# One kernel, three edits at once: LN1 reordered over eight PSUM banks, the spectral filter in three planes with its sums on VectorE, and the down weights issued after the LN2 norms

## Chip, cores, metric

One core of one Trainium2 chip. The metric is device microseconds of one execution; every time quoted is a median of runs that were all in the fast state. Profiles are single executions with the hardware profiler; their spans lie about 2 us under the timed runs. Engine names in the profile: PE is TensorE, PEld its weight loads, DVE VectorE, ACT ScalarE, POOL GpSimd, SP the engine that issues most DMAs. PS is PSUM, to whose banks the matmuls of these profiles write. "Lnnn" is a source line of the kernel that was profiled; the same statement has another number in another kernel.

## The reference

```python
h  = x + irfft2(rfft2(layernorm(x)) * (w_r + 1j*w_i))        # x: 2048 x 576, bf16
h2 = h + (gelu(n @ w_gate) * (n @ w_up)) @ w_down            # n = layernorm(h), hidden size 4608
```

## The kernel before

The kernel builds its own dependence graph: `P.op(engine, instruction, r=keys read, w=keys written)` appends an instruction to an engine's list in program order and makes it wait, by semaphores, for the last writers and readers of its keys. It runs in four stages: LN1 with the first half of the DFT along the sequence (`a_mm`, into `U`); a loop over 16 frequency groups, called D/B/V here; the inverse transform ("I") with LN2; and the gate/up and down matmuls.

The filter step of the loop, per group, complex product Y times W:

```python
# st_D(i): 6 matmuls; ACT copies the even half to ES; two DVE ops (line "CUS") make sums and differences
# st_B(i-2): 6 matmuls, ACT copies the result to YS [re, im], then:
ze = POOL if i < NG - 3 else DVE
for t_, T_, w_ in (("T1", T1, slice(0, 2)), ("T2", T2, slice(1, None, -1))):
    P.op(DVE, ... tensor_tensor(T_[:, sl], YS[:, sl], WS[:, g, w_], op=ALU.mult) ...)      # 580 elements each
for z, (t_, T_, op_) in enumerate((("T1", T1, ALU.subtract), ("T2", T2, ALU.add))):
    P.op(ze, ... tensor_tensor(ZS[:, z4, z], T_[:, sl, 0], T_[:, sl, 1], op=op_) ...)      # 290 elements each
# st_V(i-5): 6 matmuls on ZS, ACT copies the result to V
```

LN1's scale factor is multiplied into the DFT table (`ATS = ATB / std`). The 512 KB table comes in one DMA between the second and the third load of x. The weights are issued by two engines, and GpSimd's list runs in this order:

```python
... the ZS sums of the loop ...
for j in range(4):                        # gate: POOL queue, up: SP queue
    P.dma(POOL, WGU[... gate, chunk j ...]); P.dma(SP, WGU[... up, chunk j ...])
for j in range(9):
    P.dma(POOL, WD[:, 4*j:4*j+4, :], ...)                     # down weights
... in the I stage: norm(1, POOL), norm(3, POOL), then PE transposes (turn_pe) of the normed rows
```

## Time and profile before

| | before |
|---|---|
| timed median | 505.4 us (505.0 to 505.85) |
| profiled span | 503.9 us |
| first D matmul (end of LN1) | 22.49 us |
| first I matmul (end of the loop) | 56.01 us |
| loop, difference of the two | 33.52 us |
| from there to the end ("the rest") | 447.89 us |

The page of the kernel before, its chain of waits: the work that ended last, followed back, as shares of the span by engine and by line.

```profile
## 4 chain that ended last, share of the span: by engine, by line
PE 92%; DVE 4%; ACT 2%; DMA 1%; issue 1%; SPq 0%; DVEq 0%; ACTq 0%
```

TensorE holds almost all of it, and from the first I matmul on it is the limit nearly throughout. So the three times in this table decide everything here: first D, first I, and the rest. TensorE's timeline before gives them. Columns: start, duration of the merged entry, engine, line, operation, output and inputs, count, and in brackets the idle time before it and its releaser.

```profile
22.49 2.41 PE L548 MATMUL PS<-FT,U 128*128 128x290 bf16 x18 [0.35 <-DVE U L477]
...
47.12 0.91 PE L548 MATMUL PS<-FT,U 128*128 128x290 bf16 x6
...
56.01 0.41 PE L649 MATMUL PS<-DT,V 128*128 128x289 bf16 x2
```

The second line is the last D; in between, TensorE repeats every 1.91 us once all three steps run. VectorE's timeline of one group of the loop before:

```profile
28.93 0.45 DVE L554 TENSOR_TENSOR CUS<-ES,PS 128x290 bf16<-128x290 f32 x1
29.30 0.45 DVE L555 TENSOR_TENSOR CUS<-ES,PS 128x288 bf16<-128x288 f32 x1
29.66 0.45 DVE L578 TENSOR_TENSOR T_79<-YS,WS 128x580 bf16<-128x580 bf16 x1
30.03 0.92 DVE L578 TENSOR_TENSOR T_80<-YS,WS 128x580 bf16<-128x580 bf16 x1
30.88 0.45 DVE L554 TENSOR_TENSOR CUS<-ES,PS 128x290 bf16<-128x290 f32 x1
```

Read the starts, not the durations: an instruction of 0.45 us lets the next start after 0.37. The group takes 30.88 - 28.93 = 1.95 us. The second product is twice as long as the first, 0.92 us, for the same shape; GpSimd ran a sum beside it:

```profile
29.68 0.96 POOL L581 TENSOR_TENSOR ZS<-T_80 128x290 bf16<-128x290 bf16 x1
```

GpSimd's list later in the same run:

```profile
59.27 6.71 POOL L206 DMA_DIRECT2D WD<-in_B_w_down_dram  x9
66.01 6.17 POOL L715 TENSOR_SCALAR HN<-XO,TM,RS_59 128x576 bf16<-128x576 bf16 x4
```

The two norms start as soon as the nine DMAs have been issued.

### The profile page before, as it was taken

Reading aid. Unit: us, or ns where it says so; the run is one execution under the profiler, and the core shown is the slowest. Engines: PE = TensorE matmul, PEld = TensorE weight load, DVE = VectorE, ACT = ScalarE, POOL = GpSimd, SP = SyncE. Lnnn points to the kernel's source line nnn. Section 1 sums busy time; section 2 is a strip of 40 time slices with the busy share of each in tenths; the row PEclk is TensorE's granted clock in tenths of the full one; section 3 lists DMA queues with packets and bytes.
Section 4 is the critical chain, followed back from the end, with each engine's and each line's share of the span. In section 5 each row is a group of like instructions: output and inputs, shape, how many; then the busy total and the mean of one; then the engine's idle time right before and its main releaser. Section 6 shows DMA issues by size and latency. Waiting matters only on the chain.

```text
span 503.9 us, 10005 instructions
## 1 busy us (share of the span) xinstructions
PE 493.4 (98%) x4323; PEld 299.4 (59%) x4324; DVE 183.2 (36%) x382; ACT 157.1 (31%) x296; POOL 46.5 (9%) x61
## 2 busy tenths in 40 slices
PE   6899999999999999999999999999999999999998
PEld 2587675444457764444477754444577644444775
DVE  4899773344331014343310134333211233333111
ACT  5888776663220002323200022323100132323000
POOL 3278870000000000000000000000000000000000
PEclk9999999999999999999999999999999999999999
DMA  8679799001100000100000001100000000000000
GB/s 291 158 225 330 235 325 324 3 1 27 25 4 14 18 19 17 22 17 1 2 7 18 19 15 22 23 4 1 1 18 19 13 1 1 1 2 1 12 19 19
DMA packets 25661, 28.65 MB, mean 57 GB/s; under 512 B 11536, under 2 KB 19600, under 8 KB 25488
## 3 DMA queue, kind: packets, MB, share of 16 engines
q1 hardware_dynamic: 23040, 17.39, 11.9%
q0 software_dynamic: 2576, 10.62, 6.4%
q8 instruction: 34, 0.56, 0.5%
q14 instruction: 11, 0.09, 0.1%
HBM read 23.66 MB, written 2.36 MB: 52 GB/s over the span
## 4 chain that ended last, share of the span: by engine, by line
PE 92%; DVE 4%; ACT 2%; DMA 1%; issue 1%; SPq 0%; DVEq 0%; ACTq 0%
PE PS L783 56%; PE PS L806 28%; PE PS L649 2%; PE PS L548 2%; PE PS L688 2%; DMA XO<-in_A_x_dram 1%; DVE T_80 L578 1%; PE PS L568 1%; PE PS L595 1%; ACT U L479 1%; DVE T_79 L578 1%; DVE U L477 1%; DVE CUS L554 1%; ACT JNK L414 0%; DVE CUS L555 0%
## 5 line engine op out<-in xcount | busy, mean ns | idle before, releaser
L795 ACT ACTIVATE GL<-PS 128x512 bf16<-128x512 f32 x144 | 85.9, 597 | 289.3 <-PE PS L783 288.5
L796 DVE TENSOR_TENSOR AT<-GL,PS 128x512 bf16<-128x512 bf16 x144 | 98.9, 688 | 174.2 <-PE PS L783 172.5
L783 PE MATMUL PS<-HT_69,WGU 64*128 64x512 bf16 x1296 | 143.2, 376 | 0.0
L783 PE MATMUL PS<-HT_84,WGU 64*128 64x512 bf16 x1296 | 143.1, 376 | 0.0
L806 PE MATMUL PS<-WD,AT 128*128 128x288 bf16 (+2 forms) x1152 | 141.8, 286 | 0.0
L806 PEld LDWEIGHTS PS<-WD,AT 128*128 128x128 bf16 x1152 | 111.0, 98 | 31.5 <-issue 1.7
L783 PEld LDWEIGHTS PS<-HT_84,WGU 64*128 64x128 bf16 x1296 | 69.6, 94 | 71.6 <-issue 0.5
L783 PEld LDWEIGHTS PS<-HT_69,WGU 64*128 64x128 bf16 x1296 | 69.9, 94 | 70.8 <-issue 0.7
L809 DVE TENSOR_TENSOR OS<-PS,XO 128x288 bf16<-128x288 f32 (+2 forms) x32 | 14.6, 458 | 125.8 <-PE PS L806 125.8
L691 DVE SCALAR_TENSOR_TENSOR XO<-PS,XO 128x576 bf16<-128x576 f32 x16 | 12.1, 756 | 8.3 <-PE PS L688 8.3
L649 PE MATMUL PS<-DT,V 128*128 128x289 bf16 x96 | 14.6, 287 | 0.2 <-ACT V L603 0.2
L548 PE MATMUL PS<-FT,U 128*128 128x290 bf16 x96 | 14.3, 286 | 0.4 <-DVE U L477 0.4
L595 PE MATMUL PS<-VT,ZS 128*128 128x256 bf16 x96 | 13.4, 272 | 1.1 <-DVE CUS L555 0.4
L578 DVE TENSOR_TENSOR T_80<-YS,WS 128x580 bf16<-128x580 bf16 (+2 forms) x17 | 13.5, 794 | 0.0
L581 POOL TENSOR_TENSOR ZS<-T_80 128x290 bf16<-128x290 bf16 x13 | 12.2, 938 | 1.9
L606 ACT ACTIVATE V<-PS 128x768 bf16<-128x768 f32 x15 | 12.1, 810 | 0.8 <-PE PS L595 0.8
L571 ACT ACTIVATE YS<-PS 128x578 bf16<-128x578 f32 x16 | 10.5, 655 | 4.1 <-PE PS L568 3.7
L466 PE MATMUL PS<-ATS,XO 128*128 128x128 bf16 (+1 forms) x80 | 7.0, 233 | 4.6 <-POOL ATS L445 3.8
L421 DVE BATCH_NORM_STATS2 ST_53<-XO 128x6 f32<-128x288 bf16 x24 | 9.4, 442 | 4.9 <-DMA XO<-in_A_x_dram 4.9
L658 ACT ACTIVATE GS<-PS 128x578 bf16<-128x578 f32 x15 | 9.8, 654 | 4.2 <-PE PS L649 4.1
L568 PE MATMUL PS<-CUS,BT 128*128 128x289 bf16 (+2 forms) x96 | 10.8, 247 | 0.2 <-ACT YS L571 0.2
L649 PEld LDWEIGHTS PS<-DT,V 128*128 128x128 bf16 x96 | 8.9, 97 | 3.5 <-ACT V L603 0.5
(63 smaller groups left out, 190.8 us busy)
## 6 DMA issues: line engine op xcount, KB each, us to landing
WD<-in_B_w_down_dram POOLq DMA_DIRECT2D x9, 576.0 KB, 19.8
WGU<-in_B_w_up_dram SPq DMA_DIRECT2D x4, 1152.0 KB, 12.5
WGU<-in_B_w_gate_dram POOLq DMA_DIRECT2D x4, 1152.0 KB, 10.2
out_dram<-OS SPq DMA_DIRECT2D x30, 72.0 KB, 1.6
XO<-in_A_x_dram SPq DMA_DIRECT2D x3, 576.0 KB, 7.7
IT<-c_itab SPq DMA_DIRECT2D x1, 1024.0 KB, 5.5
HT_84<-HN SPq DMA_TRANSPOSE x40, 2.4
XO<-in_A_x_dram SPq DMA_DIRECT2D x2, 288.0 KB, 3.1
```

What stands on the lines that cost most here:

```text
L548: P.op(PE, lambda t, b=b, o=o, dt=dt, us=us, g=g: t.matmul(bank(b, 0, 128, 0, 2 * HK), U[:, us, g, :, :], FT[:, o, dt, :], start=(dt == 0) ...
L568: P.op(PE, lambda t, b=b, tb=tb, pl=pl, q0=q0, q1=q1, m=m, s3=s3, sp_=sp_: t.matmul(bank(b, 0, 128, q0, q1), BT[:, sp_, tb, :], CUS[:, s3, ...
L578: P.op(DVE, lambda v, g=g, sl=sl, q0=q0, q1=q1, T_=T_, w_=w_: v.tensor_tensor(T_[:, sl, :, q0:q1], YS[:, sl, :, q0:q1], WS[:, g, w_, q0:q1 ...
L581: P.op(ze, lambda v, sl=sl, z4=z4, z=z, T_=T_, op_=op_, q0=q0, q1=q1: v.tensor_tensor(ZS[:, z4, z, q0:q1], T_[:, sl, 0, q0:q1], T_[:, sl, ...
L595: P.op(PE, lambda t, b=b, o=o, c=c, zp=zp, sl=sl, sp_=sp_: t.matmul(bank(b, 0, 128, o, o + 256), ZS[:, sl, zp, 128 * c:128 * c + 128], VT[ ...
L606: P.op(ACT, lambda a, g=g, src=src: a.activation(V[:, :, :, g, :], src, ACTF.Copy), r=[("PS", bs[0]), ("PS", bs[2]), "Vfree"], w=[("V", g, ...
L649: P.op(PE, lambda t, b=b, h=h, i=i, kt=kt, c=c: t.matmul(bank(b, 0, 128, 0, K2), V[:, kt, c, :, :], DT[:, 3 * h + i, 0:K2], start=(i == 0) ...
L783: op = P.op(PE, lambda t, h0=h0, kt=kt, wt=wt, f=f, b=b, HT=HT, s=(half == 0 and j in (0, 5)), e=(half == 1 and j in (3, 8)): t.matmul(ban ...
L795: P.op(ACT, lambda a, s2=s2, b0=b0: a.activation(GL[:, s2, :], bank(b0), ACTF.Gelu_apprx_tanh), r=[("PS", b0)], w=[("GL", s2)])
L796: P.op(DVE, lambda v, s2=s2, b0=b0, f=f: v.tensor_tensor(AT[:, f, :], GL[:, s2, :], bank(b0 + 1), op=ALU.mult), r=[("GL", s2), ("PS", b0 + ...
L806: P.op(PE, lambda t, b=b, d0=d0, d1=d1, f=f, p=p: t.matmul(bank(b, 0, 128, 0, d1 - d0), AT[:, f, 128 * p:128 * p + 128], WD[:, f, d0:d1], ...
L809: P.op(DVE, lambda v, b=b, d0=d0, d1=d1, p=p, c=c: v.tensor_tensor(OS[:, p % 2, d0:d1], bank(b, 0, 128, 0, d1 - d0), XO[:, c, d0:d1], op=A ...
```

## The change

Intent: (1) start LN1 earlier and finish it sooner; (2) take GpSimd out of the filter loop, so that its sums no longer slow the products, and shorten the pipeline by one group; (3) free space and GpSimd time by loading weights in another order. With a stored plane -w_i the real part, `yr*wr - yi*wi`, becomes a sum like the imaginary part, so that one add does both. The core of the diff, with cuts (also changed, and not shown: the filter loads bring w_i before w_r, and the filler matmuls and PSUM banks of the last groups differ):

```diff
@@ x and table loads: the table in three pieces
-    for i, (c0, c1) in enumerate(((0, 2), (2, 4), (4, 8), (8, 12), (12, 16))):
-        P.dma(SP, XO[:, c0:c1, 0:D], ...)
-        if i == 1:
-            P.dma(SP, ATB[...], dram["ATAB"][:, :], "atb", w=["ATB"])
+    x_load(0, 0, 2)
+    x_load(1, 2, 4)
+    atb_load(0, 0, 4)
+    x_load(2, 4, 8)
+    atb_load(1, 4, 8)
+    x_load(3, 8, 12)
+    x_load(4, 12, 16)
+    atb_load(2, 8, 16)
@@ LN1 (cut: the whole order of its instructions is rewritten; five groups instead of six)
-        b = (5 * i + k) % 7
+        b = (5 * i + AORD.index(k) + 7) % 8
@@ st_D: wait only for the part of U that a matmul reads
-                     r=ukeys + ["FT"], w=[("PS", b)])
+                     r=uk[us] + ["FT"], w=[("PS", b)])
@@ filter: planes -w_i, w_r, w_i; one add of 580 elements on VectorE
+            for t_, w_ in enumerate((slice(1, None, -1), slice(2, 0, -1))):
+                P.op(DVE, ... tensor_tensor(TP[:, sl, t_], YS[:, sl], WS[:, g, w_], op=ALU.mult) ...)
+            P.op(DVE, ... tensor_tensor(ZS[:, z3], TP[:, sl, :, 0], TP[:, sl, :, 1], op=ALU.add) ...)
@@ before the loop: the plane -w_i
+    for i in range(NG):
+        P.op(POOL, lambda v, g=GORD[i]: v.tensor_scalar(WS[:, g, 0, :], WS[:, g, 2, :], -1.0, None, op0=ALU.mult), ...)
@@ loop: V one group sooner
-    for i in range(NG + 5):
+    for i in range(NG + 4):
...
-        if i >= 5:
-            st_V(i - 5)
+        if i >= 4:
+            st_V(i - 4)
@@ weights: the nine WD DMAs move from in front of the I stage to behind it; filter planes share
@@ memory with gate/up chunks 2 and 3, which therefore wait for the end of the filter
-    for j in range(9):
-        P.dma(POOL, WD[:, 4 * j:4 * j + 4, :], ...)
...
+    for j in range(9):
+        P.dma(POOL, WD[:, 4 * j:4 * j + 4, :], ...)
```

More of the change, by code (lines that the diff above doesn't have):

```diff
@@ L305, in _build @@
     XO = sb.alloc("XO", [128, NT, D], BF16)
-    WGU = sb.alloc("WGU", [128, 9, FF], BF16)
+    wgu_off = (sb.off + 63) // 64 * 64
+    WGU = sb.alloc("WGU", [128, 4, 9, FF // 4], BF16)
+    wgu_end = sb.off
+    sb.off = wgu_off + 2 * 9 * (FF // 4) * 2
+    WS = sb.alloc("WS", [128, NG, 3, KW], BF16)
+    sb.off = wgu_end
     HN = sb.alloc("HN", [128, 4, 640], BF16)
@@ L322, in _build @@
     U = sb.alloc("U", [128, 5, NG, NT, 8], BF16)
-    WS = sb.alloc("WS", [128, NG, 2, KW], BF16)
     CUS = sb.alloc("CUS", [128, 3, 2, KW], BF16)
@@ L350, in _build @@
     t1_off = sb.off
-    T1 = sb.alloc("T1", [128, 2, 2, KW], BF16)
-    T2 = sb.alloc("T2", [128, 2, 2, KW], BF16)
-    ZS = sb.alloc("ZS", [128, 4, 2, ZW], BF16)
+    TP = sb.alloc("TP", [128, 2, 2, 2, KW], BF16)
+    ZS = sb.alloc("ZS", [128, 3, 2, ZW], BF16)
     sb.off = t1_off
@@ L376, in _build, with x_load, atb_load @@
     ov = out[0].rearrange("(p c) d -> p c d", c=NT)
-    for i, (c0, c1) in enumerate(((0, 2), (2, 4), (4, 8), (8, 12), (12, 16))):
+    tabs = dram["ATAB"].rearrange("p (c k) -> p c k", c=NT)
+    def x_load(i, c0, c1):
         P.dma(SP, XO[:, c0:c1, 0:D], xv[:, c0:c1, :], f"x{i}", w=[("X", c) for c in range(c0, c1)])
-        if i == 1:
-            P.dma(SP, ATB[:, :, :].rearrange("p a b -> p (a b)"), dram["ATAB"][:, :], "atb", w=["ATB"])
+    def atb_load(i, c0, c1):
+        P.dma(SP, ATB[:, c0:c1, :], tabs[:, c0:c1, :], f"atb{i}", w=[("ATB", c) for c in range(c0, c1)])
+    x_load(0, 0, 2)
[6 more added lines that the diff above has]
+    atb_load(2, 8, 16)
     P.dma(SP, FT[:, :, :, :].rearrange("p a b c -> p (a b c)"), dram["FTAB"][:, :], "ft", w=["FT"])
@@ L389, in w_loads @@
         for jj in range(4):
-            o.append((WS[jj:64:4, g0:g1, pl, 1:K2], 1 + (16 * jj + g0) * K2, [[128 * K2, 16], [K2, g1 - g0], [1, K2 - 1]], jj))
-            o.append((WS[64 + jj:128:4, g0:g1, pl, 1:K2], 1 + (64 + 16 * jj + 16 - g0) * K2, [[128 * K2, 16], [-K2, g1 - g0], [1, K2 - 1]], 4 + jj))
+            o.append((WS[jj:64:4, g0:g1, 1 + pl, 1:K2], 1 + (16 * jj + g0) * K2, [[128 * K2, 16], [K2, g1 - g0], [1, K2 - 1]], jj))
+            o.append((WS[64 + jj:128:4, g0:g1, 1 + pl, 1:K2], 1 + (64 + 16 * jj + 16 - g0) * K2, [[128 * K2, 16], [-K2, g1 - g0], [1, K2 - 1]], 4 + jj))
         if hf:
             for p0 in range(2):
-                o.append((WS[64 * p0:64 * p0 + 64, 0, pl, 1:K2], 1 + 64 * p0 * K2, [[128 * K2, 16], [16 * K2, 4], [1, K2 - 1]], 8 + p0))
+                o.append((WS[64 * p0:64 * p0 + 64, 0, 1 + pl, 1:K2], 1 + 64 * p0 * K2, [[128 * K2, 16], [16 * K2, 4], [1, K2 - 1]], 8 + p0))
         return [lambda d=d, off=off, ap=ap, h=h: P.dma(eng, d, bass.AP(src.tensor, off, ap), f"w{pl}{hf}", r=["Wz"], w=[("W", hf, pl, h)]) for d, off, ap, h in o]
-    for f in w_loads(0, 0, SP) + w_loads(1, 0, SP) + w_loads(0, 1, SP) + w_loads(1, 1, SP):
+    for f in w_loads(1, 0, SP) + w_loads(0, 0, SP) + w_loads(0, 1, SP) + w_loads(1, 1, SP):
         f()
@@ L407, in _build, with act_sum, act_sq @@
     P.op(POOL, lambda g: g.memset(ZS[:, :, :, K2:ZW], 0.0), w=["Zz"])
-    GROUPS = ((0, 2), (2, 4), (4, 8), (8, 12), (12, 14), (14, 16))
-    ACT_TILES = (3, 7, 11, 13)
-    def ln1_act(c):
+    GROUPS = ((0, 2), (2, 4), (4, 8), (8, 12), (12, 16))
+    ACT_TILES = (1, 3, 7, 11, 13)
+    def act_sum(c):
         P.op(ACT, lambda a, c=c: a.activation(JNK[:, 0, :], XO[:, c, 0:D], ACTF.Identity, accum_out=SA[:, 0, c:c + 1]),
              r=[("X", c)], w=[("SA0", c), "J0"])
+    def act_sq(c):
         P.op(ACT, lambda a, c=c: a.activation(JNK[:, 1, :], XO[:, c, 0:D], ACTF.Square, accum_out=SA[:, 1, c:c + 1]),
@@ L439, in ln1_sqrt, with ln1_rs @@
              r=[("MV1", c) for c in range(c0, c1)] + ["EPT"], w=[("SD1", i)])
+    def ln1_rs(i):
+        c0, c1 = GROUPS[i]
+        P.op(DVE, lambda v, c0=c0, c1=c1: v.reciprocal(RS1[:, c0:c1], RS1[:, c0:c1]), r=[("SD1", i)], w=[("RS1", i)])
     def ln1_scale(i, eng):
         c0, c1 = GROUPS[i]
-        P.op(DVE, lambda v, c0=c0, c1=c1: v.reciprocal(RS1[:, c0:c1], RS1[:, c0:c1]), r=[("SD1", i)], w=[("RS1", i)])
         if eng == POOL:
@@ L446, in ln1_scale @@
                                                                RS1[:, c0:c1].unsqueeze(2).to_broadcast([128, c1 - c0, 128]), op=ALU.mult),
-                 r=[("RS1", i), "ATB"], w=[("ATS", c) for c in range(c0, c1)])
+                 r=[("RS1", i)] + [("ATB", c) for c in range(c0, c1)], w=[("ATS", c) for c in range(c0, c1)])
         else:
@@ L450, in ln1_scale, with a_bank, idle_mm @@
                 P.op(DVE, lambda v, c=c: v.tensor_scalar(ATS[:, c, :], ATB[:, c, :], RS1[:, c:c + 1], None, op0=ALU.mult),
-                     r=[("RS1", i), "ATB"], w=[("ATS", c)])
-    def idle_mm(n):
+                     r=[("RS1", i), ("ATB", c)], w=[("ATS", c)])
+    AORD = (0, 1, 4, 2, 3)
+    def a_bank(i, k):
+        return (5 * i + AORD.index(k) + 7) % 8
+    def idle_mm(n, i):
+        b = a_bank(i, AORD[0])
         for _ in range(n):
-            P.op(PE, lambda t: t.matmul(bank(7), ZD[:, 0:128], ZD[:, :], start=True, stop=True), r=["ZD"], w=[("PS", 7)])
+            P.op(PE, lambda t, b=b: t.matmul(bank(b), ZD[:, 0:128], ZD[:, :], start=True, stop=True), r=["ZD"], w=[("PS", b)])
     TILES = (slice(0, 256, 2), slice(256, 512, 2), slice(1, 256, 2), slice(257, 512, 2), slice(512, D))
@@ L461, in a_mm @@
         c0, c1 = GROUPS[i]
-        b = (5 * i + k) % 7
+        b = a_bank(i, k)
         w = 128 if k < 4 else 64
@@ L471, in a_ev @@
         n = c1 - c0
-        b = (5 * i + k) % 7
+        b = a_bank(i, k)
         w = 128 if k < 4 else 64
@@ L479, in a_ev, with a_mms, a_evs @@
             P.op(ACT, lambda a, s=src, d=dst: a.activation(d, s, ACTF.Copy), r=[("PS", b)], w=[("U", i, k)])
-    def a_group(i, engs, between=None, at=5):
-        for k in range(5):
+    def a_mms(i):
+        for k in AORD:
             a_mm(i, k)
-            a_ev(i, k, engs[k])
-            if k == at:
-                between()
+    def a_evs(i, eng, ks):
+        for k in ks:
+            a_ev(i, AORD[k], eng)
     P.op(ACT, lambda a: a.activation(SA[:, 0, 0:1], EPT[:, 0:1], ACTF.Sqrt), r=["EPT"], w=[("SA0", 0)])
-    A5 = (ACT,) * 5
@@ L490, in _build @@
-    ln1_act(3)
-    idle_mm(18)
+    idle_mm(11, 0)
+    act_sum(1)
+    act_sq(1)
     ln1_tile(0)
-    ln1_tile(1)
+    ln1_tile(2)
+    act_sum(3)
     ln1_var(0)
     ln1_sqrt(0)
-    ln1_act(7)
-    ln1_tile(2)
+    act_sq(3)
+    ln1_rs(0)
     ln1_scale(0, DVE)
+    a_mms(0)
     ln1_var(1)
     ln1_sqrt(1)
+    a_evs(0, ACT, (0, 1, 2, 3, 4))
+    ln1_rs(1)
+    ln1_scale(1, DVE)
+    idle_mm(2, 1)
+    a_mms(1)
     ln1_tile(4)
-    ln1_scale(1, POOL)
-    a_group(0, A5)
-    ln1_act(11)
@@ L505, in _build @@
     ln1_tile(5)
     ln1_tile(6)
+    act_sum(7)
+    act_sq(7)
+    a_evs(1, ACT, (0, 1))
     ln1_var(2)
     ln1_sqrt(2)
-    idle_mm(1)
-    a_group(1, A5)
-    ln1_act(13)
+    a_evs(1, ACT, (2, 3, 4))
     ln1_tile(8)
+    ln1_rs(2)
     ln1_scale(2, POOL)
+    idle_mm(7, 2)
+    a_mms(2)
+    act_sum(11)
+    act_sq(11)
     ln1_tile(9)
     ln1_tile(10)
+    act_sum(13)
     ln1_var(3)
     ln1_sqrt(3)
+    act_sq(13)
     ln1_tile(12)
-    ln1_var(4)
-    ln1_scale(3, POOL)
-    idle_mm(5)
@@ L522, in _build @@
-    a_group(2, A5, lambda: ln1_sqrt(4), 2)
-    ln1_tile(14)
-    ln1_scale(4, POOL)
-    ln1_tile(15)
-    ln1_var(5)
-    idle_mm(4)
-    a_group(3, (ACT, DVE, ACT, DVE, ACT), lambda: ln1_sqrt(5), 0)
-    ln1_scale(5, DVE)
-    a_group(4, (ACT, DVE, ACT, DVE, ACT))
-    a_group(5, (DVE, ACT, DVE, ACT, DVE))
-    idle_mm(2)
-    ukeys = [("U", i, k) for i in range(len(GROUPS)) for k in range(5)] + ["Uz"]
+    ln1_rs(3)
+    ln1_scale(3, POOL)
+    ln1_tile(14)
+    a_evs(2, ACT, (0, 1, 2))
+    ln1_tile(15)
@@ new lines, in _build @@
+    ln1_var(4)
+    a_evs(2, DVE, (4,))
+    ln1_sqrt(4)
+    ln1_rs(4)
+    ln1_scale(4, DVE)
+    a_evs(2, ACT, (3,))
+    idle_mm(4, 3)
+    a_mms(3)
+    a_evs(3, ACT, (0,))
+    a_evs(3, DVE, (1,))
+    a_evs(3, ACT, (2,))
+    a_evs(3, DVE, (3,))
+    a_evs(3, ACT, (4,))
+    a_mms(4)
+    a_evs(4, DVE, (0,))
+    a_evs(4, ACT, (1,))
+    a_evs(4, ACT, (2,))
+    a_evs(4, DVE, (3,))
+    a_evs(4, ACT, (4,))
+    uk = [[("U", i, k) for i in range(len(GROUPS))] + ["Uz"] for k in range(5)]
+    ukeys = [k for ks in uk for k in ks]
@@ L563, in st_B @@
         s3, sp_ = i % 3, 1 if g == 0 else 0
-        b0 = {1: 6, LAST: 2}.get(i, 4)
+        b0 = {1: 6, LAST - 1: 2}.get(i, 4)
         for b, tabs in ((b0, (0, 1, 3)), (b0 + 1, (1, 2, 0))):
@@ L571, in st_B @@
         P.op(ACT, lambda a, sl=sl, b0=b0: a.activation(YS[:, sl, :, 0:K2], banks(b0, 2, K2), ACTF.Copy), r=[("PS", b0), ("PS", b0 + 1)], w=[("Y", sl)])
-        wk = wkeys[0 if 1 <= g < 9 else 1] + ["Wz", "Yz", "Zz"]
-        z4 = i % 4
-        ze = POOL if i < NG - 3 else DVE
+        wk = wkeys[0 if 1 <= g < 9 else 1] + [("Wn", i), "Yz", "Zz"]
+        z3 = i % 3
         for q0, q1, hs in ((0, 128, (0,)), (128, KW, (1,))) if i == LAST else ((0, KW, (0, 1)),):
-            for t_, T_, w_ in (("T1", T1, slice(0, 2)), ("T2", T2, slice(1, None, -1))):
-                P.op(DVE, lambda v, g=g, sl=sl, q0=q0, q1=q1, T_=T_, w_=w_: v.tensor_tensor(T_[:, sl, :, q0:q1], YS[:, sl, :, q0:q1], WS[:, g, w_, q0:q1], op=ALU.mult),
-                     r=[("Y", sl)] + wk, w=[(t_, sl, h) for h in hs])
-            for z, (t_, T_, op_) in enumerate((("T1", T1, ALU.subtract), ("T2", T2, ALU.add))):
-                P.op(ze, lambda v, sl=sl, z4=z4, z=z, T_=T_, op_=op_, q0=q0, q1=q1: v.tensor_tensor(ZS[:, z4, z, q0:q1], T_[:, sl, 0, q0:q1], T_[:, sl, 1, q0:q1], op=op_),
-                     r=[(t_, sl, h) for h in hs], w=[("Z", z4, z, h) for h in hs])
-    VBANKS = {NG - 5: (0, 0, 1), NG - 3: (0, 0, 1), NG - 2: (4, 4, 5), LAST: (6, 7, 2)}
+            for t_, w_ in enumerate((slice(1, None, -1), slice(2, 0, -1))):
+                P.op(DVE, lambda v, sl=sl, g=g, q0=q0, q1=q1, t_=t_, w_=w_: v.tensor_tensor(TP[:, sl, t_, :, q0:q1], YS[:, sl, :, q0:q1], WS[:, g, w_, q0:q1], op=ALU.mult),
+                     r=[("Y", sl)] + wk, w=[("T", sl, t_, h) for h in hs])
+            P.op(DVE, lambda v, sl=sl, z3=z3, q0=q0, q1=q1: v.tensor_tensor(ZS[:, z3, :, q0:q1], TP[:, sl, :, 0, q0:q1], TP[:, sl, :, 1, q0:q1], op=ALU.add),
+                 r=[("T", sl, t_, h) for t_ in range(2) for h in hs], w=[("Z", z3, h) for h in hs])
+    VBANKS = {NG - 4: (0, 0, 1), NG - 2: (2, 2, 3), LAST: (0, 1, 4)}
     def st_V(i):
         g = GORD[i]
-        sl = i % 4
+        sl = i % 3
         sp_ = 1 if g == 0 else 0
@@ L596, in st_V @@
                                                                                   VT[:, sp_, zp, :], start=(zp == 0), stop=(zp == 1)),
-                     r=[("Z", sl, z, int(c > 0)) for z in range(2)] + ["Zz", "VT"], w=[("PS", b)])
+                     r=[("Z", sl, int(c > 0)), "Zz", "VT"], w=[("PS", b)])
             if i == LAST:
@@ L610, in idle_ft @@
             P.op(PE, lambda t, b=b: t.matmul(bank(b, 0, 128, 0, 2 * HK), FT[:, 0, 0, 0:128], FT[:, 0, 0, :], start=True, stop=True), r=["FT"], w=[("PS", b)])
-    P.alias(["ATB", "J0", "J1", "ZD"] + [("ATS", c) for c in range(NT)], ["Vfree"])
-    for i in range(NG + 5):
+    P.alias(["J0", "J1", "ZD"] + [(n_, c) for n_ in ("ATB", "ATS") for c in range(NT)], ["Vfree"])
+    for i in range(NG):
+        P.op(POOL, lambda v, g=GORD[i]: v.tensor_scalar(WS[:, g, 0, :], WS[:, g, 2, :], -1.0, None, op0=ALU.mult),
+             r=[k for k in wkeys[0 if 1 <= GORD[i] < 9 else 1] if k[2] == 1] + ["Wz"], w=[("Wn", i)])
+    for i in range(NG + 4):
         if i < NG:
@@ L618, in _build @@
             st_B(i - 2)
-        if i == NG + 4:
-            idle_ft(2, 3)
-        if i >= 5:
-            st_V(i - 5)
+        if i == NG + 3:
+            idle_ft(3, 5)
+        if i >= 4:
+            st_V(i - 4)
     wdv = B_w_down[:, :].rearrange("(c p) d -> p c d", p=128)
+    P.alias(wkeys[0] + wkeys[1] + ["Wz"] + [("Wn", i) for i in range(NG)], [("WG", j, k) for j in (2, 3) for k in range(4)])
     for j in range(4):
@@ L628, in _build @@
         for o, (eng, src) in enumerate(((POOL, B_w_gate), (SP, B_w_up))):
-            P.dma(eng, WGU[:, 4 * o:4 * o + 4, f0:f1], src[0:512, f0:f1].rearrange("(t p) f -> p t f", p=128), f"wgu{o}{j}", w=[("WG", j, o)])
-            P.dma(eng, WGU[64 * o:64 * o + 64, 8, f0:f1], src[512:576, f0:f1], f"wgu{o}{j}", w=[("WG", j, 2 + o)])
-    P.alias(ukeys + wkeys[0] + wkeys[1] + ["Wz", ] + [(n_, a) for n_ in ("CU", "SU") for a in range(3)], [("WD", j) for j in range(9)])
-    for j in range(9):
-        P.dma(POOL, WD[:, 4 * j:4 * j + 4, :], wdv[:, 4 * j:4 * j + 4, :], f"wd{j}", w=[("WD", j)])
+            P.dma(eng, WGU[:, j, 4 * o:4 * o + 4, :], src[0:512, f0:f1].rearrange("(t p) f -> p t f", p=128), f"wgu{o}{j}", w=[("WG", j, o)])
+            P.dma(eng, WGU[64 * o:64 * o + 64, j, 8, :], src[512:576, f0:f1], f"wgu{o}{j}", w=[("WG", j, 2 + o)])
     P.alias(["FT", "BT", "VT"], [("HT", 0, i, k) for i in range(4) for k in range(5)])
-    P.alias([("T1", a, h) for a in range(2) for h in range(2)], [("G", a, h) for a in range(2) for h in range(2)])
+    P.alias([("T", a, t_, h) for a in range(2) for t_ in range(2) for h in range(2)], [("G", a, h) for a in range(2) for h in range(2)])
     vk = [[("V", g, c) for g in range(NG)] for c in range(3)]
@@ L756, in _build @@
             turn_pe(TURN.index(c))
+    P.alias(ukeys + [(n_, a) for n_ in ("CU", "SU") for a in range(3)], [("WD", j) for j in range(9)])
+    for j in range(9):
+        P.dma(POOL, WD[:, 4 * j:4 * j + 4, :], wdv[:, 4 * j:4 * j + 4, :], f"wd{j}", w=[("WD", j)])
     fdead = vkeys + ["DT", "IT", ("G", 0, 0), ("G", 0, 1), ("G", 1, 0), ("G", 1, 1), ("Y", 0), ("Y", 1), "Yz", "Zz"]
-    fdead += [(n_, a, h) for n_ in ("T1", "T2") for a in range(2) for h in range(2)] + [("E", a) for a in range(2)]
-    fdead += [("Z", a, b_, h) for a in range(4) for b_ in range(2) for h in range(2)]
+    fdead += [("T", a, t_, h) for a in range(2) for t_ in range(2) for h in range(2)] + [("E", a) for a in range(2)]
+    fdead += [("Z", a, h) for a in range(3) for h in range(2)]
     fnew = ([("AT", f) for f in range(36)] + [("GL", 0), ("GL", 1)] + [("HT", 1, i, k) for i in range(4) for k in range(5)])
@@ L783, in gu @@
                 op = P.op(PE, lambda t, h0=h0, kt=kt, wt=wt, f=f, b=b, HT=HT, s=(half == 0 and j in (0, 5)), e=(half == 1 and j in (3, 8)): t.matmul(
-                    bank(b), WGU[h0:h0 + 64, wt, 128 * f:128 * f + 128], HT[h0:h0 + 64, kt, :], start=s, stop=e),
+                    bank(b), WGU[h0:h0 + 64, f // 9, wt, 128 * (f % 9):128 * (f % 9) + 128], HT[h0:h0 + 64, kt, :], start=s, stop=e),
                     r=[("HT", tb % 2, i, k) for i in range(4) for k in range(5)] + [("WG", f // 9, i) for i in range(4)],
```

## The prediction

> **What bounds the kernel now.** The chain of waits is 92% TensorE: 55.9% the gate/up matmuls, 28.1% the down matmuls. From 56.65 us (first inverse matmuls) to 501.5 us it is TensorE without a gap, the clock granted in full. The change leaves those matmuls alone, so about 447.8 us (503.9 - 56.1) are fixed. Only the first 56 us can move, in two stages.
>
> *LN1, 0 to 22.5 us.* The chain by time: wait for x to 8.9 us, then ScalarE without a gap (statistics, square roots, evictions) to 17.9, then VectorE to 22.35; the first D matmul starts at 22.49. ScalarE has about 3 us idle before 8.9 (its timeline), because tile 7 queues behind the 512 KB table, which lands near 7.0.
>
> *D/B/V loop, 22.5 to 56.1 us.* Timeline: TensorE repeats every 1.91 us (0.75 + 0.51 + 0.65). VectorE needs 1.945 us: two CUS ops at 0.365, T1 at 0.37, T2 at 0.85. T2 takes 0.92 in the by-line view against 0.45 for T1, because a GpSimd sum is running. The Trainium skill, "SBUF — State Buffer", section "Who interferes with whom", says a VectorE instruction with two SBUF inputs contends with a GpSimd instruction that reads SBUF; these numbers agree. So VectorE falls slowly behind. From the last D (47.87) to the end of V (56.2) takes 8.3 us for 5.4 us of TensorE work: about 2.8 us of stalls.
>
> **What the change does.**
> 1. LN1: the table in pieces puts only 128 KB ahead of tiles 4-7, so I expect these near 7.5 instead of 8.9 us and the first scaled table near 6.2 instead of 7.0. ScalarE's work grows (five tiles at 1.33 us, ten 512-wide evictions at 0.48: about 15 against 14.3 us) but starts at 3.75 without the hole. Finer U dependences let D0 start before the last two evictions. I expect D0 at 20.3 to 22, best guess 21.0: minus 1.5 us.
> 2. Sums on VectorE: one 580-element add (0.37, as T1) replaces the collision (0.47). Period 1.84 us, below TensorE's 1.91; the loop becomes TensorE-bound, lag is one group shorter. Undisturbed the stage would take about 31.7 instead of 33.6 us.
> 3. Against it: sixteen GpSimd negations of 290 elements, estimated 0.6 to 1.2 us each (its 290-element sums took 0.70). Eight fall near 16 to 23 us, when group 4's table scale runs on VectorE; eight follow the last filter load (issued near 31 us), inside the loop. Each may delay a VectorE op by about 0.5 us; slack is about 2 us per group. I take back 1 us: minus 1 us for the stage.
> 4. Gate weights are issued early instead of at 53.8 us; chunks 2 and 3 wait for the filter's end (near 52), down weights move behind the norms (about 72). First down matmul is near 147 us: not on the path, worth 0.
>
> Sum: about minus 2.5 to 3.5 us, 0.6%. Predicted 502.2 us; 80% range 500.3 to 504.8. Faster by over 2%: 0.01; within 2%: 0.98; slower: 0.01.
>
> **What would show it.** First D matmul near 21 us; T products at 0.45 in both halves outside the negations, up to 0.9 inside; TensorE from last D to first inverse matmul about 6 us instead of 8.3; first inverse matmul near 53.3; from there 447.8 us unchanged.
>
> **What would make it wrong.** Negations much slower than 1.2 us, or in front of group 4's scale, taking the whole gain; the LN1 zigzag between ScalarE and VectorE waiting at each crossing; a half-clock window (before had one, 11.7 to 15.1 us) falling on the loop; the WGU layout or late chunks stalling gate/up matmuls (would add time after 77 us).

## The result and the profile after

The changed kernel took 504.72 us (median of 4 runs, 504.17 to 505.09) against 505.6 us for the kernel before (4 runs). A ratio here is the mean time of one kernel's fast runs over that of the other's of the same rounds, so not quite the ratio of the medians: 0.9983, 95% interval 0.9966 to 1.0001. It was run again later, unaltered, with 0.9974 (0.9960 to 0.9988). The gain is about 1 us; 3.2 us had been forecast.

| us | before | after | predicted |
|---|---|---|---|
| first D matmul | 22.49 | 20.33 | 21.0 |
| first I matmul | 56.01 | 55.15 | 53.3 |
| loop | 33.52 | 34.82 | 32.3 |
| the rest | 447.89 | 447.75 | 447.8 |

LN1 gave 2.2 us, more than forecast. The loop did not get shorter by 1.2 us but longer by 1.3. The lines of TensorE's timeline after:

```profile
20.33 2.55 PE L600 MATMUL PS<-FT,U 128*128 128x290 bf16 x18 [0.54 <-DVE U L505]
...
46.72 0.91 PE L600 MATMUL PS<-FT,U 128*128 128x290 bf16 x6
...
55.15 0.28 PE L700 MATMUL PS<-DT,V 128*128 128x289 bf16 x1
```

The chain of waits after. VectorE's share rose from 4 to 6%:

```profile
## 4 chain that ended last, share of the span: by engine, by line
PE 91%; DVE 6%; issue 1%; DMA 1%; ACT 1%; DVEq 0%
```

One group on VectorE after, in a stretch without negations beside it:

```profile
27.59 0.45 DVE L606 TENSOR_TENSOR CUS<-ES,PS 128x290 bf16<-128x290 f32 x1
27.96 0.45 DVE L607 TENSOR_TENSOR CUS<-ES,PS 128x288 bf16<-128x288 f32 x1
28.32 0.83 DVE L629 TENSOR_TENSOR TP<-YS,WS 128x580 bf16<-128x580 bf16 x2
29.18 0.47 DVE L631 TENSOR_TENSOR ZS<-TP 128x580 bf16<-128x580 bf16 x1
29.56 0.45 DVE L606 TENSOR_TENSOR CUS<-ES,PS 128x290 bf16<-128x290 f32 x1
```

Both products now have their uncontended length. Yet the group takes 29.56 - 27.59 = 1.97 us, not less than before. A narrower window splits the merged entry of the two products; its second half is:

```profile
28.69 0.45 DVE L629 TENSOR_TENSOR TP<-YS,WS 128x580 bf16<-128x580 bf16 x1
```

From 28.69 to the sum at 29.18 are 0.49 us, where the other neighbours lie 0.37 apart. The sum reads what the second product writes, so it waits until that instruction has finished (28.69 + 0.45 = 29.14) and for the semaphore. That is 0.12 us in every group.

And where GpSimd's negations run beside the loop (sixteen of 0.949 us on average), a group takes longer still: 2.07 us in three groups, 2.19 in one. After, VectorE from 33.72:

```profile
33.72 0.45 DVE L606 TENSOR_TENSOR CUS<-ES,PS 128x290 bf16<-128x290 f32 x1
34.09 0.45 DVE L607 TENSOR_TENSOR CUS<-ES,PS 128x288 bf16<-128x288 f32 x1
34.45 0.82 DVE L629 TENSOR_TENSOR TP<-YS,WS 128x580 bf16<-128x580 bf16 x2
35.31 0.57 DVE L631 TENSOR_TENSOR ZS<-TP 128x580 bf16<-128x580 bf16 x1
35.79 0.45 DVE L606 TENSOR_TENSOR CUS<-ES,PS 128x290 bf16<-128x290 f32 x1
```

That is 2.07 us from CUS to CUS; of its instructions only the sum is longer, 0.57 instead of 0.47. (Which instruction pays differs: in `filter_only`, below, the two products beside negations took 1.05 us together instead of 0.83, and four groups 2.19 to 2.20.) GpSimd's late list after, against the two lines shown of before:

```profile
64.91 6.28 POOL L766 TENSOR_SCALAR HN<-XO,TM,RS 128x576 bf16<-128x576 bf16 x4 [7.71 <-DVE RS L760]
71.13 6.80 POOL L206 DMA_DIRECT2D WD<-in_B_w_down_dram  x9
```

### The profile page after: what moved, and what is told of

Same layout as the page of the kernel before. It is cut to its first block, busy times and chain, and to the rows that moved or that the text cites. A ratio compares the mean times of both kernels' runs of the same rounds, so it can differ in the third digit from the quotient of the medians.

```text
span 502.9 us, 9972 instructions
## 1 busy us (share of the span) xinstructions
PE 492.4 (98%) x4318; PEld 297.7 (59%) x4319; DVE 183.9 (37%) x391; ACT 158.7 (32%) x296; POOL 39.1 (8%) x49
## 4 chain that ended last, share of the span: by engine, by line
PE 91%; DVE 6%; issue 1%; DMA 1%; ACT 1%; DVEq 0%
PE PS L838 56%; PE PS L861 28%; PE PS L700 3%; DVE TP L629 2%; PE PS L739 2%; PE PS L600 1%; DVE ST L440 1%; DVE CUS L606 1%; PE PS L645 1%; DVE CUS L607 1%; DMA XO<-in_A_x_dram 1%; PE PS L620 1%; DVE U L505 0%; DVE ATS L472 0%; ACT JNK L431 0%
## 5 line engine op out<-in xcount | busy, mean ns | idle before, releaser
L838 PE MATMUL PS<-HT,WGU 64*128 64x512 bf16 x2592 | 281.9, 376 | 0.0
L838 PEld LDWEIGHTS PS<-HT,WGU 64*128 64x128 bf16 x2592 | 137.3, 94 | 143.4 <-issue 1.2
L665 POOL TENSOR_SCALAR WS<-WS 128x290 bf16<-128x290 bf16 x16 | 15.2, 949 | 9.3 <-DMA WS<-in_A_w_i_dram 8.2
L629 DVE TENSOR_TENSOR TP<-YS,WS 128x580 bf16<-128x580 bf16 (+2 forms) x34 | 13.5, 438 | 0.3 <-issue 0.3
L645 PEld LDWEIGHTS PS<-VT,ZS 128*128 128x128 bf16 x96 | 8.1, 97 | 4.8 <-DVE ZS L631 1.0
L600 PEld LDWEIGHTS PS<-FT,U 128*128 128x128 bf16 x96 | 9.2, 98 | 3.0 <-issue 0.7
L730 ACT ACTIVATE OS<-XO 128x576 bf16<-128x576 bf16 x16 | 10.8, 675 | 0.0
```

Of the source, the lines that this page charges most:

```text
L600: P.op(PE, lambda t, b=b, o=o, dt=dt, us=us, g=g: t.matmul(bank(b, 0, 128, 0, 2 * HK), U[:, us, g, :, :], FT[:, o, dt, :], start=(dt == 0) ...
L629: P.op(DVE, lambda v, sl=sl, g=g, q0=q0, q1=q1, t_=t_, w_=w_: v.tensor_tensor(TP[:, sl, t_, :, q0:q1], YS[:, sl, :, q0:q1], WS[:, g, w_, q ...
L645: P.op(PE, lambda t, b=b, o=o, c=c, zp=zp, sl=sl, sp_=sp_: t.matmul(bank(b, 0, 128, o, o + 256), ZS[:, sl, zp, 128 * c:128 * c + 128], VT[ ...
L665: P.op(POOL, lambda v, g=GORD[i]: v.tensor_scalar(WS[:, g, 0, :], WS[:, g, 2, :], -1.0, None, op0=ALU.mult), r=[k for k in wkeys[0 if 1 <= ...
L838: op = P.op(PE, lambda t, h0=h0, kt=kt, wt=wt, f=f, b=b, HT=HT, s=(half == 0 and j in (0, 5)), e=(half == 1 and j in (3, 8)): t.matmul(ban ...
```

## The experiments

Theory: VectorE is the loop's limit, and what the change took from it, the collision of 0.47 us, it gave back as a sum of 0.37 us plus a wait of 0.12 us for the product; negations add some half microsecond in all. Rivals: the negations are the main loss; or LN1's gain is a mere shift that the loop would lose anyway. Twelve kernels ran, each kernel five rounds beside the kernel before.

| run | median us | ratio to before | first D | first I | loop | rest |
|---|---|---|---|---|---|---|
| `ln1_only` | 504.85 | 0.9979 | 20.14 | 53.81 | 33.67 | 449.29 |
| `filter_only` | 507.07 | 1.0031 | 23.36 | 58.21 | 34.85 | 447.79 |
| `defer` | 502.94 | 0.9944 | 20.07 | 53.41 | 33.34 | 447.79 |
| `noneg` (wrong result) | 504.87 | 0.9983 | 21.12 | 55.25 | 34.13 | 447.75 |
| `ln1_wd` | 503.32 | 0.9953 | 19.94 | 53.61 | 33.67 | 447.79 |
| `sign` (wrong result) | 505.09 | 0.9988 | 20.11 | 54.45 | 34.34 | 447.75 |
| `two_sums` | 503.15 | 0.9961 | 19.86 | 54.82 | 34.96 | 447.58 |
| `defer_sign` (wrong result) | 502.64 | 0.9940 | 20.30 | 53.40 | 33.10 | 447.70 |
| `two_late` | 502.64 | 0.9938 | 19.92 | 53.21 | 33.29 | 447.59 |
| `sign_late` (wrong result) | 503.61 | 0.9957 | 19.94 | 54.08 | 34.14 | 447.72 |
| `defer_sign_late` (wrong result) | 502.03 | 0.9926 | 19.90 | 52.41 | 32.51 | 447.79 |
| `after_again` | 504.24 | 0.9974 | 19.81 | 54.53 | 34.72 | 447.77 |

The four columns on the right are from one profile each; loop is first I minus first D, and rest is the profiled span minus first I. The changed kernel's two profiles differ by 0.5 us in first D and by 0.1 in the loop, so the loop column carries finer differences than the others.

### `ln1_only`: the LN1 part alone

Edit: the kernel before with the LN1 hunks of the diff (loads of x and table, order, banks, keys of U); filter and weights as before.

> The LN1 part of the change alone (order over eight banks, table in pieces, per-bank U keys), filter and weights as before. My theory, that LN1 gained and the filter loop gave most of it back: first D matmul at 20.0 to 20.4 us as in the changed kernel (22.49 before), the loop still 33.5 us as before, first inverse matmul near 53.8, total 2.1 to 2.5 us below before (ratio near 0.9955). Rival, that LN1's gain is only a shift of the same VectorE work and the loop loses it whatever the filter looks like: first inverse matmul near 55.2, ratio near 0.998.

The first two numbers came as the theory has them: first D at 20.14, loop 33.67 us, first I at 53.81. But the total was 504.85 us, not 503. The rest took 1.4 us more than in any other kernel. TensorE in the I stage of this run:

```profile
65.69 0.44 PE L780 MATMUL PS<-IDT,HN 128*128 128x128 bf16 x5 [0.57 <-DVE HN L762]
...
69.51 0.45 PE L780 MATMUL PS<-IDT,HN 128*128 128x128 bf16 x5 [0.90 <-POOL HN L762]
```

These are the transposes of the normed rows; 0.57 + 0.90 = 1.47 us of idle time in front of two sets of them, the second released by GpSimd's norm. The first was released by VectorE's norms, two of which took 1.36 us together beside GpSimd's DMA issues (1.07 in `ln1_wd`, below). GpSimd in the same run:

```profile
59.55 6.71 POOL L206 DMA_DIRECT2D WD<-in_B_w_down_dram  x9
66.30 6.22 POOL L762 TENSOR_SCALAR HN<-XO,TM,RS 128x576 bf16<-128x576 bf16 x4
```

The norms stand behind nine DMA issues and start at 66.30 us, as they did before at 66.01, while TensorE now comes two microseconds sooner. What cost nothing before became a wait as soon as the front was shortened. This was not in my expectation.

### `ln1_wd`: LN1 and the down weights' order, filter as before

Edit, on `ln1_only`: the nine WD DMAs moved behind the I stage, as in the change.

```diff
-    for j in range(9):
-        P.dma(POOL, WD[:, 4 * j:4 * j + 4, :], ...)        # before the I stage
...
+    for j in range(9):
+        P.dma(POOL, WD[:, 4 * j:4 * j + 4, :], ...)        # after the I stage
```

> LN1 of the change plus the down weights issued behind the LN2 norms; filter as before (products on VectorE, sums on GpSimd, two planes). In the run with LN1 alone the first inverse matmul came at 53.81 us but the rest took 449.3 us instead of 447.8: TensorE waited for two transposes of normed rows, whose norms stood on GpSimd behind nine down-weight DMAs until 66.3 us. Theory: with these DMAs behind the norms the rest is 447.8 us again, first inverse matmul still near 53.8, total 1.3 to 1.6 us below LN1 alone and 2.0 to 2.4 below before (ratio near 0.9955), so also below the whole change. Rival (the gap came from the weights' transfers or from VectorE's norms): rest stays at 449.3, ratio 0.998.

As expected: the rest is 447.79 us again, the total 503.32 us, 1.5 below `ln1_only`, ratio 0.9953 (0.9936 to 0.9970). So the move of the down weights, to which the prediction gave no worth, is what lets LN1's gain reach the end, and these two parts alone are better than the whole change.

### `filter_only`: filter and weights alone

Edit: the changed kernel with the LN1 hunks undone.

> The filter in three planes and the weights' order alone, LN1 as before. Theory: first D at 22.5, the loop 1.0 to 1.4 us longer than before (VectorE period 1.965 against 1.945 us, plus about 0.5 us where negations run beside it), total 1.0 to 1.4 us above before (ratio near 1.0025). Rival (the filter is neutral, LN1's early start is what disturbs the loop): ratio 1.000.

Loop 34.85 us, 1.33 more than before, just as in the whole change; so the filter loses this with or without the new LN1. That the two loops agree to 0.03 us is partly chance: here the negations lengthened four groups, to 2.19 to 2.20 us each, and spared the first group; in the change they lengthened four to 2.07 to 2.19, and the first as well. The total rose by 1.6 us, a little above the expectation. In the profile the first D also came 0.87 us late, at 23.36. The granted clock was 0.53 between 13.3 and 20.0 us, where the kernel before had such a stretch only from 11.7 to 15.0 (0.58). LN1's part of this run is therefore not a clean comparison; the loop is.

### `defer`: the sum one instruction later

Edit: the sum of a group is issued after the next group's first CUS operation, so one other instruction stands between it and the product it reads. The last three groups keep the old order.

```diff
     P.op(DVE, ... CUS[0:HK] = e2 + o2 ...)
+    for f_ in zpend: f_()
+    zpend.clear()
     P.op(DVE, ... CUS[HK:] = e2 - o2 ...)
...
-    P.op(DVE, ... ZS = TP[:, :, 0] + TP[:, :, 1] ...)
+    zpend.append(z_sum) if i + 3 < NG else z_sum()
```

> The changed kernel with each sum issued one instruction later on VectorE, after the next group's first CUS operation, so it no longer follows directly the product it reads. Theory, that VectorE waits 0.12 us in each group for its own product: the period on VectorE falls from 1.965 to about 1.85, TensorE becomes the limit at 1.91, the stalls after the last D shrink, first inverse matmul at 52.5 to 53.5 instead of 55.15, total 1.7 to 2.7 us below the changed kernel. Rival, that the sum is simply longer than I costed or the loop is held by ScalarE or the banks: period stays at 1.96, no gain. Rival, that the negations are the whole loss: gain under 0.5 us.

VectorE in a group of this run:

```profile
26.74 0.45 DVE L608 TENSOR_TENSOR CUS<-ES,PS 128x290 bf16<-128x290 f32 x1
27.11 0.45 DVE L637 TENSOR_TENSOR ZS<-TP 128x580 bf16<-128x580 bf16 x1
27.48 0.45 DVE L612 TENSOR_TENSOR CUS<-ES,PS 128x288 bf16<-128x288 f32 x1
27.84 0.82 DVE L634 TENSOR_TENSOR TP<-YS,WS 128x580 bf16<-128x580 bf16 x2
28.58 0.45 DVE L608 TENSOR_TENSOR CUS<-ES,PS 128x290 bf16<-128x290 f32 x1
```

The same five instructions take 28.58 - 26.74 = 1.84 us instead of 1.97, the figure that the prediction had counted on. All starts are 0.37 apart. With the negations still there, the loop went from 34.82 to 33.34 us and the total to 502.94 us. The changed kernel's two medians are 1.8 and 1.3 us above that: the lower part of the expected range of 1.7 to 2.7, or 0.4 us under it. They were run at other times. The sum's own length was not the matter; its place was.

### `noneg`, `sign`, `sign_late`: without the negations

First try, `noneg`: the negations removed, the plane -w_i filled with zeros once by a GpSimd memset.

> The changed kernel without the sixteen negations (the plane of minus w_i is filled with zeros by one early memset; the result is wrong on purpose). Theory: the loop's period stays at 1.965 everywhere (with negations it was 2.07 to 2.19 in four groups), so the loop gains 0.5 to 0.7 us, group 4's table scale loses its 0.2 us hole, total 0.6 to 1.0 us below the changed kernel. Rival, that negations are the whole loss: total 2 us or more below the changed kernel.

No gain in the total, which would have spoken for neither side, for the try was spoiled: LN1 came 1 us later. VectorE and GpSimd at that place:

```profile
6.28 1.70 DVE L473 TENSOR_SCALAR ATS<-ATB,RS 128x128 bf16<-128x128 bf16 x2
```

```profile
3.93 3.97 POOL L424 MEMSET WS<- 128x4640 bf16 x1
```

The two table scales take 0.42 us together in the changed kernel. Here they take 1.70, until the memset ends at 7.90. The period in the loop was 1.97 us in every group after the first, as the theory says, and the loop of 34.13 us agrees with that of the third try, below. Second try, `sign`: no negations and no memset; both products read the loaded planes (the sign of one term is wrong).

```diff
-            for t_, w_ in enumerate((slice(1, None, -1), slice(2, 0, -1))):
+            for t_, w_ in enumerate((slice(1, 3), slice(2, 0, -1))):
```

> The changed kernel without the negations and without any memset in their place: both products read the loaded planes, the single add stays (sign of one term wrong on purpose; the earlier try without negations put a 4 us memset in front of LN1's table scale and was confounded). Theory: period 1.965 us in all groups, group 4's scale unchanged apart from 0.2 us, loop 34.0 to 34.3 us instead of 34.8, total 0.5 to 0.9 us below the changed kernel. Rival, negations are the whole loss: loop 33.0 or less.

Loop 34.34 us, first I 0.7 us earlier than in the first profile of the change, but timed runs from 503.98 to 506.90: inconclusive as a total. VectorE waited 0.6 us for filter rows in front of the first product; without negations in its list, GpSimd had issued the gate weights at 15.6 us instead of 40.2, and their transfers ran beside the filter's loads. `two_sums`, below, shows this in full. Third try, `sign_late`: the gate-weight DMAs made to wait for the filter's loads.

```diff
+                  r=wkeys[0] + wkeys[1] if eng == POOL else [],      # on the gate-weight DMAs
```

> No negations (sign wrong on purpose), single sum directly after its product, gate-weight DMAs behind the filter loads: the cost of the negations alone, without the transfers they used to hold back. Theory: period 1.965 throughout, first D near 20.1, loop 33.9 to 34.2 us, total 0.5 to 0.9 us below the changed kernel run beside it. Rival: loop 33.0 us or less, then the negations were the main cost after all.

Loop 34.14 us against 34.72 of the changed kernel run beside it (`after_again`): the negations cost 0.58 us in the loop. The timed median fell by 0.63 us. The period was about 1.97 us in all groups from the second on; two successive starts of CUS in this run:

```profile
27.05 0.45 DVE L606 TENSOR_TENSOR CUS<-ES,PS 128x290 bf16<-128x290 f32 x1
...
29.01 0.45 DVE L606 TENSOR_TENSOR CUS<-ES,PS 128x290 bf16<-128x290 f32 x1
```

The rival, that negations were the main loss, falls.

### `two_sums`, `two_late`: two planes, two short sums on VectorE

Edit: no third plane. A subtract and an add of 290 elements each, both on VectorE, behind both products. So each sum has another instruction between it and its product.

```diff
-            P.op(DVE, ... tensor_tensor(ZS[:, z3], TP[:, sl, :, 0], TP[:, sl, :, 1], op=ALU.add) ...)
+            for z, op_ in enumerate((ALU.subtract, ALU.add)):
+                P.op(DVE, ... tensor_tensor(ZS[:, z3, z], TP[:, sl, z, 0], TP[:, sl, z, 1], op=op_) ...)
```

> The changed kernel with two planes and two 290-element sums on VectorE (subtract, then add), no negations; result correct. Each sum then has one other instruction between it and its product, so nothing waits. Theory: VectorE period 4 x 0.37 + 2 x 0.22 = 1.91 to 1.93 us, equal to TensorE's; first inverse matmul at 52.6 to 53.4, total 2 to 2.6 us below the changed kernel, about as good as the deferred sum with three planes. Rival, that a sum on VectorE costs its full time whatever stands before it: period 2.03 or more, total no better than the changed kernel.

The period was 1.91 us as expected, with six instructions where the changed kernel has five in 1.97. But first I came at 54.82 us, because of one hole at the start:

```profile
25.41 0.83 DVE L629 TENSOR_TENSOR TP<-YS,WS 128x580 bf16<-128x580 bf16 x2 [2.01 <-DMA WS<-in_A_w_r_dram]
```

GpSimd, with nothing left in its list, in the same run:

```profile
15.40 2.80 POOL L206 DMA_DIRECT2D WGU<-in_B_w_gate_dram  x4
```

In the Trainium skill, "DMA: Bandwidth & Descriptors", section "Issuing engines are not separate DMA queues", DMAs of all issuing engines run on the same 16 DMA engines and interleave. The hole agrees with it, and `two_late`, which only makes the gate weights wait, tests it:

> Two planes, two sums on VectorE as in the earlier run, with GpSimd's first gate-weight DMAs made to wait for the filter loads. Without negations in front of them these DMAs went out near 16 us, and the first product waited 2.0 us for filter rows. Theory: the hole in front of the first product goes, period stays 1.91 us, first inverse matmul at 52.5 to 53.2 (was 54.8), total about 502.0 to 502.6 us, 1 us below LN1 with the weights' order or better. Rival, that the rows were late because their loads are issued in another order: the hole stays.

```profile
23.80 0.83 DVE L629 TENSOR_TENSOR TP<-YS,WS 128x580 bf16<-128x580 bf16 x2 [0.34 <-ACT YS L623]
```

The wait for the DMA is gone, the loop takes 33.29 us, and the total is 502.64 us (502.51 to 502.79), ratio 0.9938 (0.9926 to 0.9951). First I came at 53.21, at the edge of the expected range. This kernel is correct and the fastest correct one, 1.6 us below the changed kernel run beside it. `defer` was as good within the intervals (0.9944, 0.9932 to 0.9956).

### `defer_sign`, `defer_sign_late`: the loop with its costs taken away

Edits: the deferred sum and no negations (sign wrong), without and with the gate weights held back.

> Deferred sum and no negations (sign wrong on purpose): both costs of the filter taken away. Theory: VectorE needs 1.845 us a group and TensorE's 1.91 is the limit; first D at 20.0, last D ends near 45.9, first inverse matmul at 52.0 to 52.8; 0.6 to 1.2 us below the deferred sum alone. If the two costs don't add (TensorE-bound either way), equal to the deferred sum within 0.3 us.

`defer_sign` had the same hole, 0.93 us in front of the first product, and reached 53.40 us, no better than `defer`. This is what the second clause of the expectation allowed, but for a cause that it does not name.

> Deferred sum, no negations (sign wrong on purpose), gate-weight DMAs behind the filter loads: the filter with none of its three costs. Theory: VectorE 1.845 us a group, TensorE 1.91 and the limit; first D near 20.1, loop 31.7 to 32.3 us as I had predicted for the undisturbed change, first inverse matmul near 52.1, total 2.8 to 3.4 us below the changed kernel. Rival, another limit (banks, ScalarE): loop above 33 us.

```profile
45.29 0.91 PE L602 MATMUL PS<-FT,U 128*128 128x290 bf16 x6
...
49.24 0.81 PE L655 MATMUL PS<-VT,ZS 128*128 128x256 bf16 x6 [0.20 <-DVE ZS L637]
50.38 0.83 PE L655 MATMUL PS<-VT,ZS 128*128 128x256 bf16 x6 [0.33 <-DVE ZS L637]
...
52.41 0.28 PE L708 MATMUL PS<-DT,V 128*128 128x289 bf16 x1
```

TensorE now ran the groups at its own 1.91 us, VectorE at 1.84. The loop took 32.51 us, a little above the expected range, and the total was 502.03 us, 2.2 below the changed kernel beside it, not the expected 2.8 to 3.4. From the start of the last D to the first I matmul are 7.1 us; in the change they are 8.4. TensorE did not become the limit even here. VectorE's timeline shows no idle time from its first product at 23.79, 3.9 us after the first D, to its copy of V at 51.84, and in the last groups TensorE waits for its sums (0.20 and 0.33 us). At 0.07 us a group VectorE did not make up its lag within the sixteen groups.

### `after_again`: the changed kernel, unaltered, beside the last three

> The changed kernel once more, unaltered, beside the three above on one chip. Same as on its first run: ratio to before 0.9983 within 0.001, first D near 20.3, loop 34.8 us.

Ratio 0.9974, loop 34.72 us: as on its first run within the stated tolerance; first D came at 19.81 instead of 20.33.

## Why the prediction was wrong

The step that failed reads: "one 580-element add (0.37, as T1) replaces the collision (0.47). Period 1.84 us, below TensorE's 1.91; the loop becomes TensorE-bound". I had costed the add by the start-to-start time of neighbours that do not depend on each other. Placed right behind its product it costs 0.37 + 0.12 us. Thus 0.49 us replaced the collision of 0.47. VectorE stayed the limit at 1.965 us a group, and the loop lost the negations' cost on top. The second half of the step failed too: with the period of 1.84 us reached (`defer_sign_late`), VectorE still ended last, because it starts behind TensorE and sixteen groups are too few to catch up. A period below TensorE's does not by itself make the loop TensorE-bound.

Without the negations the loop was still 0.62 us longer than before (`sign_late`, 34.14 against 33.52), though the period grew by only 0.02 us. Most of that, 0.49 us, lies in the first group: from its third to its fourth CUS operation VectorE took 2.41 us instead of 1.92. Before, no GpSimd sum was running when the first group's second product started, and it took 0.46 us; so there the new sum had no collision to replace.

The loop in numbers, each from a difference of two runs: 34.72 (changed) less 0.58 for the negations (`sign_late`, 34.14) less 1.63 for the wait (`defer_sign_late`, 32.51). The 1.63 us agree with 13 deferred groups at 0.12 to 0.13 us: in both runs VectorE's timeline shows no other gap between its first product and its copy of V, so all that it saves reaches the end. The prediction had 31.7 undisturbed plus 1.0 for the disturbance; its forecast of the first I matmul, 53.3 less 21.0, makes it 32.3. The terms compare so:

- Wait for the own product: predicted 0, measured 1.63 us. This alone is most of the missing gain.
- The undisturbed loop: predicted 31.7 with TensorE as the limit, measured 32.51 with VectorE ending last.
- The negations: predicted 1 us of loss for the stage, measured 0.58; the mechanism was right, the size too large. Their length, 0.949 us, lay within the forecast 0.6 to 1.2.
- LN1: predicted 21.0, measured 20.33 and 19.81; right in direction, with about 1 us more gain than forecast. As forecast, ScalarE's hole is gone: it was idle for 2.88 us before 8.90, after the change, from its first statistic at 3.84 on, for 0.50 us at most (before 7.30) in that stretch. Which of the LN1 edits gave how much was not timed.
- Weights: "not on the path, worth 0" was wrong. Without the move, LN1's gain of 2.3 us shrinks by 1.5 us in the rest (`ln1_only` against `ln1_wd`). I had looked only at when the weights are needed, and not at which norms stand behind their issue on GpSimd. In the whole change this wait does not appear, so it made no error in the total: 447.8 was right.

The total by profile: first D 0.67 us earlier than forecast, loop 2.5 us longer, hence 1.85 us late at the first I matmul. The gain was 0.9 us, and 1.4 us in the second run, where 3.2 had been forecast. The theory of a VectorE-bound loop with a wait for its own result was tested from both sides: remove the wait and the period falls to 1.84 (`defer`); remove the negations and it stays at 1.97 (`sign_late`). What stays open: whether the whole change without the weights' move would show the full 1.5 us wait (not run), and why first D moves by 0.5 us between the two profiles of the changed kernel: 0.3 us of it is there at ScalarE's first statistic, which waits for x until 3.84 in one and 3.54 in the other; the rest is not explained.

## What to carry to other kernels

Cost an instruction by where it stands, not only by what it is: behind the instruction whose result it reads, the 0.37 us of independent neighbours became 0.49 here, and moving it one place took that back. Compare not only periods but where each engine starts: VectorE, with the shorter period, still ended last. When a part of a program is made earlier, look at every engine's list for work that was just in time before, for it may be the next wait; and when an engine's list is emptied, look at which DMAs it will issue earlier, and what these will run beside. A change of several parts should be timed in parts: here two of three made the kernel 2.2 us faster, and the third took about half of it back.

## What the Trainium skill lacked or had wrong

- "VectorE: DVE Perf Modes", section "The DRAIN you can't avoid" and the rules at its end ("Minimize op *count*, not sems") say, from a measured row of eight copies, that a semaphore between chained instructions costs nothing extra. (The section adds that a next instruction which is not held starts earlier, without a time.) Here independent neighbours started 0.37 us apart (an instruction of 0.45 us) and a sum that waited for its product 0.49 us after it; six instructions without such a wait took 1.91 us, five with it 1.97.
- "SBUF — State Buffer", section "Who interferes with whom": the exclusive lock agrees with two runs. A product took 0.92 instead of 0.45 us beside a GpSimd sum, and two table scales took 1.70 instead of 0.42 us until a GpSimd memset of 3.97 us ended. But beside GpSimd negations (one input, about 1 us each, back to back) a group with three two-input VectorE instructions grew only from 1.97 to 2.07 us (2.19 in one), in the groups of 2.07 with the two products at their normal length; in `filter_only` it grew to 2.19 to 2.20. A full block by each negation would be expected to cost more. The page does not say what makes this milder.
- No page has the time of a one-input bf16 instruction of 290 elements on GpSimd; it was 0.949 us on average, where two-input sums of the same size took 0.70 to 0.96.
